# Factors ahead of the sum, gathers and the eighth load ahead of the key copies, and no drain on GpSimd's queue: attention and a routed mixture of experts on one core

## Chip, cores and metric

The kernel runs on one core of one Trainium2 chip. The metric is the device time of one execution in microseconds (us). The engines are TensorE (PE, matmuls and transposes; PEld is its weight load), VectorE (DVE), ScalarE (ACT), GpSimd (POOL) and SyncE (SP), which only issues DMAs here. GpSimd issues DMAs too: the casting loads of weights, the gathers and scatters by index, and some stores.

## What is computed

Blockwise causal attention over 8 batches, 8 heads, 576 positions and 64 features, then a layer of experts. Every position picks one of 8 experts, or, by a local gate, keeps the expert of the position before it.

```python
scores = np.where(block_i >= block_j, scale * q @ k.T, -1e9)     # blocks of 64
x = softmax(scores) @ v                                           # (8, 576, 512)
logits = x @ w_gate                                               # (8, 576, 8)
local_gate = sigmoid(x @ w_local)
for b, s:
    fresh_e = argmax(logits[b, s])
    e = fresh_e if s == 0 or local_gate[b, s] < 0.5 else prev_e
    h = relu(x[b, s] @ w1[e])                                     # 512 -> 1024
    out[b, s] = softmax(logits[b, s])[e] * (h @ w2[e])            # 1024 -> 512
```

## The kernel before

**Attention, 32 pairs.** The main loop (L1201) takes two heads at a time: 4 pairs a batch, 32 pairs, numbered from 0. Iteration i does on TensorE the value products of pair i−1 (L1000, L1009, tile `o`), the scores of pair i (L979, `sc`) and the transposes of the keys and queries of pair i+1 (L695, tile `kq`). ScalarE makes the exponentials `S` and `Pc`. VectorE adds the chunks of `Pc` to `S` (`add_chunks`, L1021 and L1023), so that one product with `sel` gives the row sums; a memset of a corner of `S` (`mask`, L1028) goes ahead of that product. `half_batch` (L708, tile `trg`) makes gate products (with `wg`) and these sums (with `sel`) for two pairs at a time.

**Keys.** `load_qk(i + 2)` (L869) issues the loads of keys and queries on SyncE's queue into a staging area; `arrange(i + 2)` (L882) copies each of the two, on GpSimd, into another part of that area, from which the transposes read. The areas are the places of the last two second-layer weights, experts 6 and 7. Even and odd pairs take turns, but pairs 29, 30 and 31 all use the last one, as expert 6 is loaded by then. So the loads of pair 31 wait until the copies of pair 30 have read.

**Routing.** While pairs run, VectorE and TensorE work through a generator of steps (`early`, L1056) with weights; `vector` lets it run as many VectorE steps as the numbers in AHEAD_OF, AFTER and END allow, and `END` is the credit at the end of an iteration by its number modulo 4. For the first five batches (groups 0 and 1) it computes each position's expert and rank (`tokens`), the probability of the expert (`factors_of`, L402) and then (`slots_first`, L456) the indices `idx0` of 15 tiles of 128 rows, each for one expert. These sums by one-hots run through L518 and L521 on VectorE and L531 on TensorE, at pair 28.

**Rows.** The attention's rows, divided by their sums (`rows_of_batch`, L821), are staged in `xg` or `x` and stored to `x_rows` in memory; each row has its factor in a last column, stored by separate DMAs from `factors` (L1255) that are kept in a list `held_f`. The six buffers of `xg` are also where the gathers (L653) bring a tile's rows. The list `pending` holds the first four gathers and the load of the eighth expert's first layer (L107); it is emptied on GpSimd at the end of iteration 28. The second layer of that expert (L111) is loaded at the end of iteration 30.

**Experts, 38 tiles.** 15 tiles come from the first five batches (phase 0), 23 and a conditional few from all that is left (phase 1). Per tile: a gather on GpSimd, a transposing DMA on SyncE's queue (`xT`, L1372), a copy of the expert's first layer on VectorE (`w1c`, L1359; for tiles 0 and 1 L1082), 32 matmuls (`ps_h`, L1097), relu, 8 matmuls (`ps_y`, L1303), scaling, and a scatter (L1314). Tile i's second product stands behind tile i+1's first. Beside tiles 1 to 13 the routing of the last three batches runs in the same way (`late`, L1322): `point` is called three times a tile and adds EACH to a credit. The indices `idx1` of phase 1 are its end, and the gather of tile 15, the first of phase 1, waits for that.

All engines run their instructions in the order in which the program lists them; semaphores make them wait for one another. DMAs issued by GpSimd share one queue.

Of the kernel before, what the change touches and what calls it, by code (L numbers as in the profile page):

```python
# [62 lines left out]
def kernel(  # L63
# [11 lines left out]
    nc = tc.nc  # L75
# [11 lines left out]
    E = moe_w_gate.shape[1]  # L87
# [27 lines left out]
    HP = H // 2  # L115
# [340 lines left out]
    def slots_first(T, TM, A):  # L456
# [82 lines left out]
                       + [lambda: load_weights(E - 1, 0)])  # L539
        nc.vector.tensor_copy(pay[:, NT:, ROW1], row1[:, 0, ns:])  # L540
        yield "V", 0.6
        yield from factors_of(*GROUPS[1], TM)
        yield "V", 0.6
        experts_of(0, te, TX)
        yield "V", 1.3

# [285 lines left out]
    with tc.tile_pool(name="atn_const", bufs=1) as cst, \  # L832
# [223 lines left out]
        def early():  # L1056

            while clock[0] < 4:
                yield None
            yield from constant_steps(T1)  # L1060
            yield "V", 1
            for j in range(2):

                while clock[0] < HP * GROUPS[j][1] // NC + 1.5:
                    yield None
                c0, c1 = GROUPS[j]
                TT = scratch_of_weights(0, E - 2)
                yield from tokens(c0, c1, TT, (TT, M1)[j], A1[:, c0:c1])
                if j == 0:
                    yield "V", 0.7  # L1070
                    yield from factors_of(c0, c1, TT)
            yield "V", 1
            yield from slots_first(S1, M1, A1)

# [72 lines left out]
        wload = 0  # L1147


        AHEAD_OF, AFTER, END = (0.6, 0.4, 0.4, 0.8), (0.4, 0.8, 0.4, 1.4), (1.7, 1.6, 1.5, 1.8)  # L1150

        left = [0]

# [22 lines left out]
        def behind(i):  # L1176

            def between():
                if i % HP == 2 and i < NPAIR - 2 or not routing(i) and i > 1:
                    vector(AHEAD_OF[i % HP])  # L1180
                run(sums)
                if sums:
                    routing(i)

            sums = sums_of(i)
            if sums:
                values(i - 1, between)
            else:
                values(i - 1)
                between()  # L1190
            if not swap:
                add_chunks(i - 1)
            if i == NPAIR - 2:
                mask(i - 1, nc.vector)
            load_v(i + 1)
            if i > 1:
                vector(AFTER[i % HP])
# [3 lines left out]
        for i in range(NPAIR):  # L1201
# [45 lines left out]
                routing(i)  # L1247
            if i < NPAIR - 1:
                vector(END[i % HP])
            arrange(i + 2, [nc.gpsimd.tensor_copy] * 2)  # L1250
            if i != NPAIR - 2:
                mask(i - 1, nc.gpsimd)
            for dst, src, made in held_f[:2 if i < HP * (NB1 + 2) else None]:
                if made < i or i == HP * (NB1 + 2):
                    nc.sync.dma_start(out=dst, in_=src)  # L1255
                    held_f.pop(0)
            if pending and i >= HP * (NB1 + 2):
                release(queue=nc.gpsimd)
            while pending and i >= HP * (NB1 + 2):
                pending.pop(0)()  # L1260

            if wload < 2 * E - 2 and i == min(2 + 2 * wload, HP * (NB1 + 2) - 1):
                load_weights(*divmod(wload, 2))
                wload += 1
            if i < NPAIR - 1:
                release(queue=nc.gpsimd)
            if i == NPAIR - 2:

                free = bf(Sb[(NPAIR - 3) % NSB], 2 * S * 2)[:, -AHEAD * Dm:]
                xTs = {}  # L1270
                for j in range(AHEAD):
                    xTs[j] = free[:, j * Dm:(j + 1) * Dm].rearrange("p (k n) -> p k n", k=KO1)
                    nc.sync.dma_start(out=xTs[j], in_=row_of_x(xgs[j]), transpose=True)
                load_weights(E - 1, 1)
        assert not pending
        clock[0] = NPAIR
        release()
        holding[0] = False


        nc.gpsimd.drain()

        values(NPAIR - 1)
        half.clear()
# [10 lines left out]
    with tc.tile_pool(name="ffn_s", bufs=2, reuse_waits="tile") as f_p, \  # L1295
# [54 lines left out]
                points[0] = 0  # L1350
            credit[0] -= spent

        EACH, ROWS_AT = 0.8, 4
        credit, points = [0], [0]
        chain, others = Steps(late()), Steps(rows())
        def weights_of(i):
# [136 lines left out]
```

## Time and profile before

| | us |
|---|---|
| median of 3 runs | 410.55 |
| lowest, highest | 410.48, 417.23 |
| the profiled execution | 411.95 |
| its span, first to last instruction | 409.9 |

The profile is of one execution. A row of the order of time has start, duration, engine, line, operation, what is written and read, count, and in brackets how long the engine was idle before it and what ended that. In a row of waits stand the engine and line that waited, what for, the total in us, how often, and the longest. A row of a stretch has start and end, then the busy us of PE, PEld, DVE, ACT and POOL with counts, the granted TensorE clock (1.00 is full), the DMA engines' share and GB/s. In the stretch from 0 to 240 us TensorE is busy almost throughout; 240 to 250 has it busy for 6.93 us at a mean clock of 0.83, 310 to 320 for 7.71 at 0.95. The profile names both layers' weights `w_bf`, both index tables `idx`.

### The profile page before, as it was taken

The numbers are of one execution on the slowest core, as the hardware profiler recorded it, in microseconds if no ns is written. First come the engines' busy times: TensorE is split into PE (matmuls) and PEld (weight loads), VectorE is DVE, ScalarE is ACT, GpSimd is POOL, SyncE is SP. The second block draws the span as 40 slices with busy tenths as digits, with TensorE's granted clock in tenths as the row PEclk, the third lists the DMA queues.
The fourth block names the chain that finished last, engine by engine and source line by source line (L and its number), as shares of the span: only waits on it lengthen the run. The fifth ranks groups of instructions, "written<-read, shape, count | busy, mean of one in ns | idle before, by whom it ended". The sixth has DMA issues, their size and how long they took to land. (4 is left out here: it accounts for less than half of the span.)

```text
span 409.9 us, 14501 instructions
## 1 busy us (share of the span) xinstructions
PE 393.1 (96%) x5827; PEld 285.4 (70%) x5827; DVE 239.0 (58%) x468; ACT 226.8 (55%) x390; POOL 187.2 (46%) x240
## 2 busy tenths in 40 slices
PE   8999999999999999998999979999998999999975
PEld 7677777776776776766777647677775777777753
DVE  3443756547577886469799646787894234433220
ACT  4667666665666665557556645444454355555442
POOL 1345255144154163341443272176866567766613
PEclk9999999999999999999999999999999899999998
DMA  6589999998988979989899979677552744565432
GB/s 182 135 191 231 206 175 240 203 185 227 214 162 236 203 155 201 187 193 217 157 211 224 180 171 173 116 138 176 138 153 87 157 143 130 150 149 142 125 88 78
DMA packets 111539, 69.97 MB, mean 171 GB/s; under 512 B 77567, under 2 KB 102975, under 8 KB 111472
## 3 DMA queue, kind: packets, MB, share of 16 engines
q0 software_dynamic: 18880, 34.83, 41.4%
q1 hardware_dynamic: 92592, 34.20, 35.4%
q8 instruction: 48, 0.79, 0.8%
q14 instruction: 19, 0.16, 0.1%
HBM read 66.88 MB, written 14.70 MB: 199 GB/s over the span
## 5 line engine op out<-in xcount | busy, mean ns | idle before, releaser
L882 POOL COPY w_bf<-w_bf 128x512 f32<-128x512 f32 x61 | 48.6, 812 | 106.8 <-DMA w_bf<-in_k_dram 75.5
L1021 DVE TENSOR_TENSOR S<-S,Pc 128x896 f32<-128x896 f32 (+2 forms) x96 | 84.7, 882 | 20.5 <-PE o L1000 16.0
L979 PE MATMUL sc<-qkT 64*64 64x224 f32 (+6 forms) x1536 | 90.1, 364 | 0.0
L1359 DVE COPY w1c<-w_bf 128x4096 bf16 x36 | 44.7, 1246 | 59.4 <-PE ps_h L1097 34.2
L1097 PEld LDWEIGHTS <-w1c 128*128 128x128 bf16 x1152 | 68.1, 98 | 12.6 <-issue 5.8
L1100 ACT ACTIVATE hT<-ps_h 128x512 bf16<-128x512 f32 x76 | 44.7, 598 | 52.2 <-PE ps_h L1097 32.3
L1303 PE MATMUL ps_y<-w_bf,hT 128*128 x304 | 72.4, 382 | 0.3 <-issue 0.3
L1097 PE MATMUL ps_h<-xT,w1c 128*128 128x128 bf16 x1088 | 67.8, 220 | 4.5 <-DMA xT<-xg 2.3
L979 PEld LDWEIGHTS sc<-qkT 64*64 64x64 f32 x1536 | 70.0, 133 | 1.2 <-ACT Pc L989 0.2
L653 POOL DMA_INDIRECT xg<-x_rows,idx x38 | 50.3, 1324 | 43.3 <-issue 17.8
L989 ACT ACTIVATE Pc<-sc 128x448 f32<-128x448 f32 (+1 forms) x96 | 68.2, 715 | 1.2 <-issue 1.1
L1314 POOL DMA_INDIRECT out_dram<-y,idx x38 | 46.0, 1210 | 26.1 <-issue 9.4
L1000 PE MATMUL o<-Pc,v 128*64 128x320 f32 (+2 forms) x512 | 57.4, 366 | 0.0
L1000 PEld LDWEIGHTS o<-Pc,v 128*64 128x64 f32 x512 | 35.3, 137 | 23.4
L989 ACT ACTIVATE S<-sc 128x576 f32<-128x576 f32 x64 | 42.0, 656 | 12.2 <-PE sc L979 12.2
L1303 PEld LDWEIGHTS <-hT 128*128 128x128 bf16 x304 | 28.6, 99 | 28.6 <-issue 1.8
L1311 ACT ACTIVATE y<-ps_y,xg 128x512 f32<-128x512 f32 (+1 forms) x38 | 25.9, 683 | 25.5 <-PE ps_y L1303 19.0
L1013 ACT COPY oT<-o 128x576 f32<-128x576 f32 x32 | 20.5, 641 | 34.1 <-PE o L1009 34.0
L1000 PE MATMUL o<-S,v 128*64 128x192 f32 (+1 forms) x256 | 34.8, 392 | 1.1 <-ACT Pc L989 0.8
L717 ACT COPY LT<-trg 128x320 f32<-128x320 f32 x15 | 6.4, 426 | 48.6 <-PE trg L708 48.6
L821 DVE TENSOR_TENSOR xg<-trx,rs 128x512 bf16<-128x512 f32 (+1 forms) x31 | 20.2, 684 | 19.3 <-PE trx L695 19.0
L948 ACT COPY qkT<-kq 128x1024 f32<-128x1024 f32 x30 | 30.8, 1028 | 0.4 <-PE kq L695 0.4
(273 smaller groups left out, 424.1 us busy)
## 6 DMA issues: line engine op xcount, KB each, us to landing
w_bf<-in_moe_w_dram POOLq DMA_DIRECT2D x16, 1024.0 KB
w_bf<-in_k_dram SPq DMA_DIRECT2D x32, 256.0 KB
w_bf<-in_q_dram SPq DMA_DIRECT2D x32, 256.0 KB
v<-in_v_dram SPq DMA_DIRECT2D x64, 128.0 KB
x_rows<-xg POOLq DMA_DIRECT2D x24, 128.0 KB
qkl<-in_k_dram SPq DMA_DIRECT2D x32, 32.0 KB
qkl<-in_q_dram SPq DMA_DIRECT2D x32, 32.0 KB
vl<-in_v_dram SPq DMA_DIRECT2D x32, 32.0 KB
```

Source lines behind the costliest of these rows:

```text
L653: st = nc.gpsimd.indirect_dma_start(out=x, out_offset=None, in_=x_dram[:rows], in_offset=bass.IndirectOffsetOnAxis(ap=row_of(ph, j), axis= ...
L882: copies[j](m, raws[i][1 + j].rearrange("p h j d -> p j h d"))
L948: nc.scalar.copy(to.rearrange("p a (r s) -> p r a s", r=2), ps.rearrange("p r (a s) -> p r a s", a=2))
L979: nc.tensor.matmul(to[:, col + skip:col + n], lhsT=t[r, 0, k0:k0 + ST], rhs=t[r, 1, q0 + skip:q0 + n], start=True, stop=True)
L989: nc.scalar.activation(exps_at(i, c, q0, n, rows), ps[rows, :, col:col + n], func=AF.Exp, scale=scale_attn)
L1000: nc.tensor.matmul(po[64 * h:64 * h + 64, VO + q0:VO + q0 + n], lhsT=vs[i][c][:, h, :], rhs=exps_at(i, c, q0, n, slice(0, P))[:, h, :], st ...
L1021: nc.vector.tensor_add(Ss[i][:, :, P * c:], Ss[i][:, :, P * c:], Pc[i % 2][:, :, POS[c]:POS[c] + n])
L1097: nc.tensor.matmul(ps[:, fo, :], lhsT=w[:, ko * F + f0:ko * F + f0 + P], rhs=xT[:, ko, :], start=(ko == 0), stop=(ko == KO1 - 1))
L1100: relu[0] = nc.scalar.activation(hT[:, half * (FO // 2):(half + 1) * (FO // 2), :], ps, func=AF.Relu)
L1303: nc.tensor.matmul(ps, lhsT=hT[:, fo, :], rhs=w2_bf[:, bass.ds(ev + fo * Dm, Dm)], start=(fo == 0), stop=(fo == FO - 1))
L1314: st = nc.gpsimd.indirect_dma_start(out=out_flat, out_offset=bass.IndirectOffsetOnAxis(ap=row_of(ph, j), axis=0), in_=y, in_offset=None, b ...
L1359: ended["w"] = nc.vector.tensor_copy(w, w1_bf[:, bass.ds(ev[i], WE)])
```

## The change

- The factors of group 1 (batches 3 and 4) are computed right behind its tokens, ahead of `slots_first`, and not behind the sum that gives the first indices. Their four stores go out two by two at the ends of iterations 26 and 27.
- At the end of each iteration the memset goes ahead of the key copies on GpSimd. For iterations 28 to 30 it is VectorE's, behind the chunk sums.
- At the end of iteration 28 the row store, the four gathers and the load of the eighth expert's first layer go ahead of the copies of pair 30.
- The load of that expert's second layer goes ahead of the row stores of iteration 30.
- No drain ahead of the last values. END has 2.4 for 1.6, EACH 1.0 for 0.8.

```diff
         nc.vector.tensor_copy(pay[:, NT:, ROW1], row1[:, 0, ns:])
         yield "V", 0.6
-        yield from factors_of(*GROUPS[1], TM)
-        yield "V", 0.6
         experts_of(0, te, TX)
...
                 yield from tokens(c0, c1, TT, (TT, M1)[j], A1[:, c0:c1])
-                if j == 0:
-                    yield "V", 0.7
-                    yield from factors_of(c0, c1, TT)
+                yield "V", 0.7
+                yield from factors_of(c0, c1, (TT, M1)[j])
             yield "V", 1
             yield from slots_first(S1, M1, A1)
...
-        AHEAD_OF, AFTER, END = (0.6, 0.4, 0.4, 0.8), (0.4, 0.8, 0.4, 1.4), (1.7, 1.6, 1.5, 1.8)
+        AHEAD_OF, AFTER, END = (0.6, 0.4, 0.4, 0.8), (0.4, 0.8, 0.4, 1.4), (1.7, 2.4, 1.5, 1.8)
...
-            if i == NPAIR - 2:
+            if HP * (NB1 + 2) <= i < NPAIR - 1:
                 mask(i - 1, nc.vector)
...
-            arrange(i + 2, [nc.gpsimd.tensor_copy] * 2)
-            if i != NPAIR - 2:
+            if i < HP * (NB1 + 2) or i == NPAIR - 1:
                 mask(i - 1, nc.gpsimd)
-            for dst, src, made in held_f[:2 if i < HP * (NB1 + 2) else None]:
-                if made < i or i == HP * (NB1 + 2):
-                    nc.sync.dma_start(out=dst, in_=src)
-                    held_f.pop(0)
             if pending and i >= HP * (NB1 + 2):
                 release(queue=nc.gpsimd)
             while pending and i >= HP * (NB1 + 2):
                 pending.pop(0)()
+            arrange(i + 2, [nc.gpsimd.tensor_copy] * 2)
+            for dst, src, made in held_f[:2]:
+                if made < i:
+                    nc.sync.dma_start(out=dst, in_=src)
+                    held_f.pop(0)
+            assert i < HP * (NB1 + 2) or not held_f
...
                 load_weights(*divmod(wload, 2))
                 wload += 1
+            if i == NPAIR - 2:
+                load_weights(E - 1, 1)
             if i < NPAIR - 1:
                 release(queue=nc.gpsimd)
...
-                load_weights(E - 1, 1)
...
-        nc.gpsimd.drain()
...
-        EACH, ROWS_AT = 0.8, 4
+        EACH, ROWS_AT = 1.0, 4
```

The order on GpSimd from the end of iteration 27 to the end of iteration 30, before. `xg_97` is the tile `xg`, `x_4028` and `x_4030` are two buffers of `x`, and the copies are the key copies of pairs 30 and 31:

```order
L680 DMA x_rows<-xg_97 128x256 x2
L882 COPY w2_bf_59<-w2_bf_59 128x512 x2
L1028 MEMSET S_104 64x2x64
L680 DMA x_rows<-xg_97 64x256
L653 DMA xg_97<-x_rows,idx0_89 128x257 x4
L107 DMA w1_bf_58<-in_moe_w1_dram 128x4x1024
L882 COPY w2_bf_59<-w2_bf_59 128x512 x2
L1028 MEMSET S_104 64x2x64
L680 DMA x_rows<-x_4028 128x256
L680 DMA x_rows<-x_4030 128x256
L680 DMA x_rows<-xg_97 64x256
L111 DMA w2_bf_59<-in_moe_w2_dram 128x8x512
```

The same place after the change (its lines are numbered two lower):

```order
L678 DMA x_rows<-xg_97 128x256 x2
L678 DMA x_rows<-xg_97 64x256
L651 DMA xg_97<-x_rows,idx0_89 128x257 x4
L107 DMA w1_bf_58<-in_moe_w1_dram 128x4x1024
L880 COPY w2_bf_59<-w2_bf_59 128x512 x4
L111 DMA w2_bf_59<-in_moe_w2_dram 128x8x512
L678 DMA x_rows<-x_4028 128x256
L678 DMA x_rows<-x_4030 128x256
L678 DMA x_rows<-xg_97 64x256
```

Both pairs' key copies now stand behind the gathers and the load, the two memsets have left GpSimd, and the load from `in_moe_w2` stands ahead of the stores from `x`.

Further down the same queue, where phase 1 begins: the scatters of tiles 8 to 12 (`y` with its number, then the index table) and the first gathers by `idx1`, before:

```order
L1314 DMA out_0_dram<-y_4900,idx0_89 4608x512
L1314 DMA out_0_dram<-y_4971,idx0_89 4608x512
L1314 DMA out_0_dram<-y_5040,idx0_89 4608x512
L1314 DMA out_0_dram<-y_5126,idx0_89 4608x512
L653 DMA xg_97<-x_rows,idx1_90 128x257 x4
L1314 DMA out_0_dram<-y_5209,idx0_89 4608x512
```

and after, where `y_4922` is tile 8's:

```order
L1311 DMA out_0_dram<-y_4922,idx0_89 4608x512
L1311 DMA out_0_dram<-y_5006,idx0_89 4608x512
L651 DMA xg_97<-x_rows,idx1_90 128x257 x2
L1311 DMA out_0_dram<-y_5084,idx0_89 4608x512
L651 DMA xg_97<-x_rows,idx1_90 128x257
L1311 DMA out_0_dram<-y_5146,idx0_89 4608x512
```

The first gathers of phase 1 have moved from behind tile 11's scatter to behind tile 9's.

On VectorE, around the chunk sums of pair 26 (L1021, L1023) and up to the sums that give `idx0`, before:

```order
L518 TENSOR_TENSOR w1_bf_58<-io_r_75,w1_bf_58 128x240
L1021 TENSOR_TENSOR S_104<-S_104,Pc0_117 128x2x448
L1021 TENSOR_TENSOR S_104<-S_104,Pc0_117 128x2x320
L1021 TENSOR_TENSOR S_104<-S_104,Pc0_117 128x2x192
L1023 TENSOR_TENSOR S_104<-S_104 64x2x64
L521 TENSOR_TENSOR x_f_3487<-w1_bf_58,row1s_85 128x480
```

and after:

```order
L1019 TENSOR_TENSOR S_104<-S_104,Pc0_117 128x2x448
L1019 TENSOR_TENSOR S_104<-S_104,Pc0_117 128x2x320
L1019 TENSOR_TENSOR S_104<-S_104,Pc0_117 128x2x192
L1021 TENSOR_TENSOR S_104<-S_104 64x2x64
L518 TENSOR_TENSOR w1_bf_58<-io_r_75,w1_bf_58 128x240
L521 TENSOR_TENSOR x_f_3494<-w1_bf_58,row1s_85 128x480
```

The first one-hot (L518) has moved behind the chunk sums.

## The prediction

> **What bounds the kernel now.** I read the page first, then what TensorE waits for, then the order of time around those waits.
>
> ```profile
> span 409.9 us, 14501 instructions
> PE 393.1 (96%) x5827; PEld 285.4 (70%) x5827; DVE 239.0 (58%) x468; ACT 226.8 (55%) x390; POOL 187.2 (46%) x240
> ```
>
> TensorE (PE) is busy for 96% of the span, and the change takes no matmul away. So it can win only what TensorE idles, and what it runs at a lowered clock. The table of waits has three entries above 1 us for PE:
>
> ```profile
> PE trg L708 <- POOL S L1028: 3.5, 3, 3.1
> PE ps_h L1097 <- DMA xT<-xg: 2.3, 1, 2.3
> PE ps_h L1097 <- ACTq L1453: 2.2, 1, 2.2
> ```
>
> The third is at the extra-tile branch near the end, which isn't touched. The other two lie where the change works. The order of time on TensorE shows each, with a later undisturbed run of the same sums (261.93) for comparison:
>
> ```profile
> 233.98 0.66 PE L695 MATMUL kq<-id_f,w_bf 64*128 64x64 f32 x16
> 240.52 0.75 PE L708 MATMUL trg<-oT,wg 128*32 128x320 f32 x8
> 244.33 2.36 PE L708 MATMUL trg<-S,sel 128*32 128x320 f32 x16 [3.07 <-POOL S L1028]
> 246.79 0.90 PE L695 MATMUL kq<-id_f,w_bf 64*128 64x64 f32 x16
> ...
> 261.93 1.28 PE L708 MATMUL trg<-S,sel 128*32 128x320 f32 x16
> ...
> 318.24 2.88 PE L1097 MATMUL ps_h<-xT,w1c 128*128 128x128 bf16 x32 [2.29 <-DMA xT<-xg]
> 320.91 2.65 PE L1303 MATMUL ps_y<-w_bf,hT 128*128 x8
> 323.40 1.95 PE L1097 MATMUL ps_h<-xT,w1c 128*128 128x128 bf16 x32
> 325.19 1.89 PE L1303 MATMUL ps_y<-w_bf,hT 128*128 x8
> ```
>
> Both gaps cost more than their idle time, because the granted clock halves behind them (start, us, five engines, then clock):
>
> ```profile
> 244.00:245.00 1.00, 0.67 (x8) 0.33 (x12) 0.00 (x0) 0.00 (x0) 0.22 (x2) 0.50 0.58 70
> 319.00:320.00 1.00, 1.00 (x14) 1.00 (x12) 0.00 (x0) 0.00 (x0) 0.69 (x2) 0.52 0.83 197
> ```
>
> **What it can win.** Gap A, before the sums of pair 30: 3.07 idle, 2.36 − 1.28 = 1.08 on the sums and 0.90 − 0.66 = 0.24 on the key transposes, 4.4 us. Gap B, before tile 15: 2.29 idle, 2.88 − 1.95 = 0.93 and 2.65 − 1.89 = 0.76, 4.0 us. The two small waits for the same memset, 3.5 − 3.1 = 0.4 us. In all 8.8 us.
>
> Gap A goes because the memset of pair 28's sums moves to VectorE, ahead of the work that GpSimd does for the gathers. Gap B goes because a larger credit (EACH) ends the routing chain two tiles earlier: the first two phase-1 gathers stand behind the output of tile 9 instead of tile 11, and a tile takes at most 1.95 + 1.89 = 3.8 us by the last two rows above, so they come some 7 us earlier, against 2.29 us of lateness. Next in line are the later gathers, each with a tile's time behind the one before.
>
> **What it costs, part by part.** GpSimd in order of time, before:
>
> ```profile
> 218.29 0.91 POOL L111 DMA_DIRECT2D w_bf<-in_moe_w_dram  x1 [0.34 <-PE trx L695]
> 220.42 1.14 POOL L680 DMA_DIRECT2D x_rows<-xg  x2 [1.22 <-DVE xg L821]
> 226.49 0.62 POOL L882 COPY w_bf<-w_bf 128x512 f32<-128x512 f32 x1 [4.93 <-DMA w_bf<-in_k_dram]
> 228.69 0.72 POOL L882 COPY w_bf<-w_bf 128x512 f32<-128x512 f32 x1 [1.58 <-DMA w_bf<-in_q_dram]
> ...
> 235.94 1.10 POOL L653 DMA_INDIRECT xg<-x_rows,idx  x1 [5.68 <-DMA x_rows<-factors]
> 237.34 1.84 POOL L653 DMA_INDIRECT xg<-x_rows,idx  x1 [0.30 <-issue]
> ...
> 240.98 1.00 POOL L653 DMA_INDIRECT xg<-x_rows,idx  x1 [0.31 <-issue]
> 241.98 0.83 POOL L107 DMA_DIRECT2D w_bf<-in_moe_w_dram  x1
> 242.86 1.17 POOL L882 COPY w_bf<-w_bf 128x512 f32<-128x512 f32 x2
> 244.08 0.20 POOL L1028 MEMSET S<- 64x128 f32 x1
> ...
> 252.08 0.93 POOL L111 DMA_DIRECT2D w_bf<-in_moe_w_dram  x1
> ...
> 264.43 1.59 POOL L653 DMA_INDIRECT xg<-x_rows,idx  x1 [11.06 <-issue]
> ```
>
> *The factors earlier.* On SyncE's queue their four stores now go two by two ahead of the key loads of pairs 29 and 30; those loads, in place for 226.49 until now, are next wanted at 235.6 (below), so this is hidden. The wait of 5.68 us goes, and the first gather can start soon after its indices:
>
> ```profile
> 222.77 0.17 DVE L452 TENSOR_SCALAR idx<-x_f 128x15 int32<-128x15 f32 x1
> ```
>
> But the third and fourth gather write xg[2] and xg[3], from which the two stores issued at 220.42 still read, and those stand in GpSimd's DMA queue behind the 1 MB load issued at 218.29. What that queue moved in 213 to 222 and in 223 to 231 us (packets, MB, share):
>
> ```profile
> q0 software_dynamic: 609, 1.28, 79.2%
> ...
> q0 software_dynamic: 1080, 1.20, 81.1%
> ```
>
> In the first stretch an earlier load and two stores (1.05 + 0.26 = 1.31 MB) go through; in the second 1.20 MB of the next load and its two stores, again 1.31 MB. At 1.20 / 8 = 0.15 MB per us the rest needs until 231.8, and the third gather starts at about 232.3 (between 231 and 233.5), however early the first two ran.
>
> *The key copies behind the gathers.* Behind the third gather (1.0 to 1.84, I take 1.2) come a gap of 0.30, the fourth (1.0), the load (0.83) and only then the two key copies of pair 30 (0.62, 0.72): 232.3 + 1.2 + 0.3 + 1.0 + 0.83 + 0.62 = 236.2, and 236.9. TensorE wants them at 233.98 and would be through at 234.6; now it is through at 236.9 + 0.33 = 237.2. Loss 2.6, I take 3.0 for what one semaphore adds on either side (1.6 to 4.9 by the ends above). Before, these copies were made at 226 to 229, and hidden.
>
> *The clock behind this new gap.* Gap B's 2.29 us was enough for a halved clock, so I add gap A's 1.08 + 0.24 = 1.3 (0 to 1.7, gap B's). The Trainium skill, "TensorE: Matmul & The Clock Gate", section "Part 1: The HAM clock gate", has the clock fall after an idle window of about 3.4 us; by that no 3-us gap would halve it, and the sum would be 1.3 less. The trace disagrees with its 2.29.
>
> *The keys of pair 31.* Their loads wait for those copies, since both pairs use one staging area:
>
> ```profile
> 216.44 1.07 SPq L869 DMA_DIRECT2D w_bf<-in_k_dram  x1
> ...
> 232.58 1.33 SPq L869 DMA_DIRECT2D w_bf<-in_k_dram  x1
> ```
>
> They are issued at 236.2 instead of 232.58, just behind a 1 MB load instead of ahead of it. The nearest loads in such company are pair 30's: 216.44 to 226.49, 10.05 us. So k lands at 246.3 and the q copy ends at 236.9 + 10.05 + 0.7 = 247.6. TensorE comes there at 237.2, plus 244.33 − 3.07 − 234.6 = 6.6 of work, 1.28 of sums and 1.3 of slow clock: 246.4. Loss 1.0 (0 if the loads take under 9 us; 3.4 if two more).
>
> *The eighth load ahead of the row stores.* It now waits for pair 31's transposes (246.79 + 0.90) and goes ahead of the stores of x: 247.7 + 0.93 + 1.05/0.15 + 0.9 + about 1.5 for start and receipt = 258. VectorE's next rows write those same two buffers, at
>
> ```profile
> 255.19 1.28 DVE L821 TENSOR_TENSOR x<-trx,rs 128x512 bf16<-128x512 f32 x2
> 256.39 1.22 DVE L1082 COPY qkT<-w_bf 128x4096 bf16 x1
> 257.52 2.60 DVE L1021 TENSOR_TENSOR S<-S,Pc 128x896 f32<-128x896 f32 x3
> ...
> 260.04 1.96 PE L1097 MATMUL ps_h<-S,qkT 128*128 128x128 bf16 x32
> ```
>
> so they, and behind them on VectorE the copy of tile 1's weights and the last sums, come 2.8 later. The copy then ends at 260.4, tile 1 waits 0.4, and the sums for trg (261.93) another 1.3. Loss 1.7 (0 to 4, since the transposes of the first gathered tiles now also run beside that load).
>
> *Small ones.* One one-hot (L518) falls behind pair 26's sums, on the way to the first gathers' indices:
>
> ```profile
> 213.77 0.41 DVE L518 TENSOR_TENSOR w_bf<-io_r,w_bf 128x240 bf16<-128x240 f32 x1
> ```
>
> at most 0.41, I take 0.3. With EACH at 1.0 the chain crowds VectorE, busy 9.17 us (the third engine) of these ten:
>
> ```profile
> 280.00:290.00 10.00, 10.00 (x110) 7.16 (x108) 9.17 (x22) 5.26 (x9) 6.89 (x6) 1.00 0.64 141
> ```
>
> I take 0.4 (0 to 1). The drain is free: GpSimd's 11.06 idle us ahead of 264.43 hold nobody up on TensorE. The memsets ahead of the key copies, pair by pair, only trade places on an engine that waits for keys; END's larger credit likewise moves work within VectorE's idle time.
>
> Losses 3.0 + 1.3 + 1.0 + 1.7 + 0.3 + 0.4 = 7.7 against 8.8: 1.1 us faster. The profiled execution took 411.95, its span 409.9 and 2.05 around it; the median of the runs is 410.55, 1.4 lower. 411.95 − 1.1 = 410.85 there, and 409.5 on the scale of the median.
>
> **The rivals.**
> 1. *The stores of xg land early, or the copies aren't late.* Then new gap, clock and keys (5.3) fall away: 404.2, and 402.5 if the x buffers are free in time too (both stores late is one cause, the queue's rate), 401.8 if the small costs are nothing. For it: GpSimd idled 4.93 us ahead of 226.49, which the gathers would fill, and 0.15 MB per us was measured beside other traffic. Against it: the queue is busy at 81% of the engines in that stretch as it is. 0.28, of it 0.17 at 2% or past it.
> 2. *The keys of pair 31 come late* (slower than before). From a load time of 9 us on, each us is lost on TensorE; at 13, with a second halved clock, 3.9 + 1.3 instead of 1.0: 413.7. 0.18, a third of it with further waits behind, past 2%. For it: in 213 to 222 us, while a load of 2 KB rows ran, the queue of the keys moved little:
>
> ```profile
> q1 hardware_dynamic: 1126, 0.45, 22.1%
> ```
>
> The Trainium skill, "DMA: Bandwidth & Descriptors", section on queues, rings and completion order, has each DMA engine take turns between queues packet by packet. By that page 1 KB packets beside 2 KB ones get a third of the (1.28 + 0.45) / 9 = 0.19 MB per us, an estimate of 8 us for the 0.52 MB of both keys, short of that point.
>
> 3. *The clock stays up behind the new gap*: 1.3 less, 408.2. 0.09; the row of gap B speaks against it. It is also what the Trainium skill's rule in "TensorE: Matmul & The Clock Gate" would give.
> 4. *The chain isn't earlier*, because VectorE at 9.17 of 10 can't be fed faster: gap B stays, 413.5. 0.09.
>
> **How the numbers follow.** The forecast, new stalls in the place of the old ones, has 0.36. Rivals 1 to 4 make up the rest. Its own range, with the two largest terms at their ends, is 406 to 413. The range 402 to 415 takes in rival 1 and rivals 2 and 4 each alone; it leaves out the two together and what is worse, some 0.15. 2% (8.2 us) is about what a measurement of this kernel can tell from no change; 8.8 us of gain just reach it, with rival 1's 0.17. Slower by as much needs rival 2's last third, or rival 4 on top: 0.09. Within: 0.74.
>
> **What would show it.** Right: no idle ahead of trg near 244; an idle of some 3 us ahead of kq near 234, put down to a copy on GpSimd, whose third gather starts behind 231; a half clock after it; w1c, tile 1, late by 1 to 2 us; no wait for xT at tile 15. Wrong: all four gathers issued by 229, or the key copies of pair 30 done before 234; then rival 1 holds. A second gap ahead of the next kq is rival 2.

## The result and the profile after

| | median, us | runs | ratio to the kernel before, 95% interval |
|---|---|---|---|
| before | 413.89 | 410.48, 410.55, 417.23, 420.18 | |
| changed | 425.67 | 425.05, 425.34, 426.00, 428.14 | 1.038 [1.031, 1.045] |
| changed, on another chip (f0 below) | 427.24 | 423.22 to 431.55 | 1.029 [1.018, 1.040] |

Disturbed runs, two of the four of e1 among them, are left out of every ratio and of the medians of the kernel before that are given with the experiments. The kernel is slower by 3 to 4%, where the forecast was 1 us faster. The profiled execution took 426.0, its span 424.2; that of before was 409.9. From the page of the changed kernel:

```profile
span 424.2 us, 14452 instructions
PE 397.0 (94%) x5806; PEld 290.8 (69%) x5827; DVE 231.4 (55%) x470; ACT 225.7 (53%) x390; POOL 172.5 (41%) x238
```

The table of waits of the changed kernel. Neither the memset (3.5 us before) nor `xT` (2.3) is in it any more; the two at the top are new.

```profile
PE kq L693 <- POOL w_bf L880: 6.5, 1, 6.5
PE trg L706 <- DVE x L819: 4.0, 1, 4.0
PE ps_h L1094 <- ACTq L1450: 2.3, 1, 2.3
```

The order of time on TensorE, changed kernel: the first wait ahead of the keys of pair 30, no wait for those of pair 31 (255.17), the second wait, tile 1 at half clock, and tile 15 (331.36) with no wait.

```profile
237.10 0.24 PE L693 MATMUL o<-id_f,qkl 64*128 64x64 f32 x1 [0.15 <-DMA qkl<-in_k_dram]
238.17 0.27 PE L693 MATMUL o<-id_f,qkl 64*128 64x64 f32 x1 [0.83 <-DMA qkl<-in_q_dram]
244.96 1.24 PE L693 MATMUL kq<-id_f,w_bf 64*128 64x64 f32 x16 [6.51 <-POOL w_bf L880]
255.17 0.66 PE L693 MATMUL kq<-id_f,w_bf 64*128 64x64 f32 x16
...
271.58 0.75 PE L706 MATMUL trg<-oT,wg 128*32 128x320 f32 x8 [4.00 <-DVE x L819]
272.94 3.42 PE L1094 MATMUL ps_h<-S,qkT 128*128 128x128 bf16 x32 [0.62 <-DVE qkT L1079]
...
327.85 1.95 PE L1094 MATMUL ps_h<-xT,w1c 128*128 128x128 bf16 x32
331.36 1.95 PE L1094 MATMUL ps_h<-xT,w1c 128*128 128x128 bf16 x32
```

Laying the starts of the same instructions of the two profiles side by side gives the account of the 14.3 us. "Late" is the changed kernel's start less that of before; each row's share is the growth of that lateness.

| up to | late, us | share | what lies in it |
|---|---|---|---|
| scores of pair 1 | 1.55 | +1.55 | first loads, ahead of anything the change touches |
| scores of pair 29 | 3.01 | +1.46 | a wait of 1.18 for `qkl`, 0.72 for the one-hots of L521, others |
| scores of pair 30 | 12.79 | +9.78 | waits of 0.15, 0.83 and 6.51, then a halved clock |
| scores of pair 31 | 8.15 | −4.64 | gap A is gone |
| tile 1 | 12.90 | +4.75 | waits of 4.00 and 0.62 |
| tile 2 | 13.97 | +1.07 | tile 1 at half clock |
| tile 14 | 15.57 | +1.60 | tiles 6 to 11 later by 1.9, part given back |
| tile 16 | 11.48 | −4.09 | gap B is gone |
| end | 14.26 | +2.78 | 1.65 of it a halved clock that fell on the extra tile |

So both gains came in this execution, each to 0.2 us as forecast. The losses add up to 23 us, where 7.7 was forecast. The first and the last row are mostly luck: all profiles of the experiments are between 0.4 us early and 1.8 late at pair 1, and from tile 16 to the end they gain up to 0.9 or lose up to 3.7. The wait of 2.3 us at the extra tile was there before too (2.2), without a halved clock behind it. Without these two rows the losses are 18.7 us. GpSimd in order of time shows where the largest begins:

```profile
214.99 0.80 POOL L107 DMA_DIRECT2D w_bf<-in_moe_w_dram  x1
...
223.36 0.62 POOL L880 COPY w_bf<-w_bf 128x512 f32<-128x512 f32 x1 [2.34 <-DMA w_bf<-in_k_dram]
227.52 0.86 POOL L880 COPY w_bf<-w_bf 128x512 f32<-128x512 f32 x1 [3.54 <-DMA w_bf<-in_q_dram]
228.33 0.91 POOL L111 DMA_DIRECT2D w_bf<-in_moe_w_dram  x1
229.23 1.62 POOL L678 DMA_DIRECT2D x_rows<-xg  x3
...
232.56 1.02 POOL L651 DMA_INDIRECT xg<-x_rows,idx  x1 [0.30 <-issue]
241.15 1.00 POOL L651 DMA_INDIRECT xg<-x_rows,idx  x1 [7.57 <-DMA x_rows<-xg]
...
244.25 1.20 POOL L880 COPY w_bf<-w_bf 128x512 f32<-128x512 f32 x2
...
257.48 0.94 POOL L111 DMA_DIRECT2D w_bf<-in_moe_w_dram  x1 [3.08 <-PE trx L693]
```

The load of expert 6's second layer (L111) was issued at 218.29 before and is issued at 228.33 here. The two stores behind it (L678) land late with it, the third gather waits 7.57 for them, and the key copies of pair 30 stand behind that gather. The load is late because it stands behind the key copies of pair 29 (223.36 and 227.52; before 214.32, two in 2.48). SyncE's queue tells why those came late:

```profile
213.42 1.96 SPq L1256 DMA_DIRECT2D x_rows<-factors  x2
215.48 0.54 SPq L867 DMA_DIRECT2D w_bf<-in_k_dram  x1
216.11 0.41 SPq L867 DMA_DIRECT2D w_bf<-in_q_dram  x1
```

The loads of pair 29 go out at 215.48, behind two factor stores and half a us behind the issue of a 1 MB load (214.99 above). Before, they went out at 210.22, 2.2 us ahead of that load (212.39). Here are SyncE and then GpSimd of the kernel before:

```profile
210.22 0.54 SPq L869 DMA_DIRECT2D w_bf<-in_k_dram  x1
...
212.39 0.80 POOL L107 DMA_DIRECT2D w_bf<-in_moe_w_dram  x1
...
214.32 2.48 POOL L882 COPY w_bf<-w_bf 128x512 f32<-128x512 f32 x2
```

Of the 5.3 us by which the loads go out later, about 3 are TensorE's own lateness at pair 27 and 2 are the stores. From issue to copy the keys take 7.9 us instead of 4.1, and the queries 11.4.

Behind the 6.51 us the clock is halved, as forecast; it fell while TensorE still waited:

```profile
242.00:243.00 1.00, 0.00 (x0) 0.00 (x0) 0.00 (x0) 0.00 (x0) 0.70 (x2) 0.50 0.13 31
```

### The profile page after: what moved, and what is told of

It is laid out like the page before. It is cut to its first block, busy times and chain, and to the rows that moved or that the text cites. A ratio compares the mean times of both kernels' runs of the same rounds, so it can differ in the third digit from the quotient of the medians.

```text
span 424.2 us, 14452 instructions
## 1 busy us (share of the span) xinstructions
PE 397.0 (94%) x5806; PEld 290.8 (69%) x5827; DVE 231.4 (55%) x470; ACT 225.7 (53%) x390; POOL 172.5 (41%) x238
## 4 chain that ended last, share of the span: by engine, by line
PE 49%; issue 19%; POOL 14%; DMA 9%; DVE 5%; ACT 1%; POOLq 1%; SPq 1%; DVEq 0%; ACTq 0%
PE o L998 16%; PE sc L977 15%; POOL out_dram L1311 8%; PE trg L706 5%; POOL xg L651 5%; PE kq L693 3%; DMA v<-in_v_dram 3%; DMA x_rows<-x 3%; DVE S L1019 2%; DMA out_dram<-y,idx 2%; DMA w_bf<-in_q_dram 2%; PE o L1007 2%; PE ps_h L1094 2%; PE trx L693 1%; PE ps_y L1300 1%
## 5 line engine op out<-in xcount | busy, mean ns | idle before, releaser
L1019 DVE TENSOR_TENSOR S<-S,Pc 128x896 f32<-128x896 f32 (+2 forms) x96 | 80.1, 835 | 22.3 <-PE o L998 17.8
L977 PE MATMUL sc<-qkT 64*64 64x224 f32 (+6 forms) x1536 | 91.4, 367 | 0.0
L1094 PEld LDWEIGHTS <-w1c 128*128 128x128 bf16 x1152 | 68.1, 99 | 12.6 <-issue 4.5
L1300 PE MATMUL ps_y<-w_bf,hT 128*128 x283 | 68.4, 382 | 1.2 <-issue 0.2
L1026 POOL MEMSET S<- 64x128 f32 x28 | 5.6, 200 | 120.1 <-DVE S L1021 62.0
L1311 POOL DMA_INDIRECT out_dram<-y,idx x38 | 43.7, 1149 | 24.8 <-ACT y L1308 13.2
L880 POOL COPY w_bf<-w_bf 128x512 f32<-128x512 f32 x61 | 38.3, 650 | 36.7 <-DMA w_bf<-in_k_dram 21.3
L998 PEld LDWEIGHTS o<-Pc,v 128*64 128x64 f32 x512 | 36.7, 138 | 22.6 <-issue 0.6
L998 PE MATMUL o<-S,v 128*64 128x192 f32 (+1 forms) x256 | 35.9, 400 | 1.5 <-DMA v<-in_v_dram 1.0
```

Source lines behind the costliest of these rows:

```text
L880: copies[j](m, raws[i][1 + j].rearrange("p h j d -> p j h d"))
L977: nc.tensor.matmul(to[:, col + skip:col + n], lhsT=t[r, 0, k0:k0 + ST], rhs=t[r, 1, q0 + skip:q0 + n], start=True, stop=True)
L998: nc.tensor.matmul(po[64 * h:64 * h + 64, VO + q0:VO + q0 + n], lhsT=vs[i][c][:, h, :], rhs=exps_at(i, c, q0, n, slice(0, P))[:, h, :], st ...
L1019: nc.vector.tensor_add(Ss[i][:, :, P * c:], Ss[i][:, :, P * c:], Pc[i % 2][:, :, POS[c]:POS[c] + n])
L1094: nc.tensor.matmul(ps[:, fo, :], lhsT=w[:, ko * F + f0:ko * F + f0 + P], rhs=xT[:, ko, :], start=(ko == 0), stop=(ko == KO1 - 1))
L1300: nc.tensor.matmul(ps, lhsT=hT[:, fo, :], rhs=w2_bf[:, bass.ds(ev + fo * Dm, Dm)], start=(fo == 0), stop=(fo == FO - 1))
```

## The experiments

The kernels whose labels begin with e, c or f are the changed kernel with edits, those with b the kernel before with edits. They ran on several chips, and the kernel before ran beside them: its median was 411.05 beside e1 to e4, 412.27 beside e5, c1, c3 and b4, 416.08 beside e7, b1, b2 and b3, and 412.40 beside f0 to f3. So ratios are to be compared, not times.

**The keys of pair 30.** Four kernels ask whether the order on GpSimd makes the wait, and what makes its input late.

e1: the copies ahead of the gathers again.

```diff
+            arrange(i + 2, [nc.gpsimd.tensor_copy] * 2)
             if pending and i >= HP * (NB1 + 2):
                 release(queue=nc.gpsimd)
             while pending and i >= HP * (NB1 + 2):
                 pending.pop(0)()
-            arrange(i + 2, [nc.gpsimd.tensor_copy] * 2)
```

> The changed kernel with the two key copies of pair 30 ahead of the row store, the four gathers and the load again, as before; nothing else is undone. Theory A (the copies only stand in the wrong place in GpSimd's order: bytes on the key queue say that pair 30's keys had landed by about 231.5, and they were copied at 244.25): the copies come by 233, the idle time ahead of kq of pair 30 falls from 6.51 to under 1.0, no halved clock behind it, time 415 to 419 in place of 425.7. Theory B (the loads of those keys are themselves late beside the load of expert 6's second layer, so the order does not matter): copies after 238, at least 3 us idle ahead of kq, time 421 to 426.

It took 415.50 and 415.76. GpSimd and TensorE of e1:

```profile
233.39 1.32 POOL L880 COPY w_bf<-w_bf 128x512 f32<-128x512 f32 x1 [8.13 <-DMA w_bf<-in_k_dram]
235.63 0.83 POOL L880 COPY w_bf<-w_bf 128x512 f32<-128x512 f32 x1 [0.91 <-DMA w_bf<-in_q_dram]
```

```profile
237.80 0.71 PE L693 MATMUL kq<-id_f,w_bf 64*128 64x64 f32 x16
```

The copies follow the landing, and TensorE does not wait at all. Theory A: about 4.6 us over the kernel before are left of some 14. The copies are at 233.39 and 235.63 though, later than A's 233: the loads are not quick either.

e7: the two stores ahead of the second-layer load of iteration 27.

```diff
+            if i == HP * (NB1 + 2) - 1:
+                release(queue=nc.gpsimd)
             if wload < 2 * E - 2 and i == min(2 + 2 * wload, HP * (NB1 + 2) - 1):
                 load_weights(*divmod(wload, 2))
```

> The changed kernel with one pair swapped on GpSimd: the two stores from xg[2] and xg[3] in iteration 27 ahead of the 1 MB load of expert 6's second layer, not behind it. Theory A (the third gather waits only for those stores, and they only for that load): the third gather follows the second at once, at 233 to 235 in place of 241.15, the key copies of pair 30 come by 238, idle ahead of kq of pair 30 at most 2.0 in place of 6.5, time 416 to 420. Theory B (the stores land late for another reason): third gather after 238, time 422 to 427.

419.95 (417.47 to 424.92), ratio 1.011 [0.998, 1.024]. GpSimd of e7:

```profile
224.83 0.92 POOL L111 DMA_DIRECT2D w_bf<-in_moe_w_dram  x1
...
231.84 1.13 POOL L651 DMA_INDIRECT xg<-x_rows,idx  x1 [0.30 <-issue]
233.28 1.40 POOL L651 DMA_INDIRECT xg<-x_rows,idx  x1 [0.30 <-issue]
...
237.01 1.21 POOL L880 COPY w_bf<-w_bf 128x512 f32<-128x512 f32 x2
```

The third gather follows the second at once, and kq of pair 30 has no wait. Theory A: gather behind stores, stores behind the load. (The second copy ends at 238.22, where A had 238.)

f0: the changed kernel once more, on the chip of f1.

> The changed kernel once more, as the neighbour of the other three on the same chip. Both theories: 424 to 428, the third gather 12 to 14 us behind the issue of expert 6's second-layer load, and idle time ahead of kq of pair 30 of 3 to 7 us.

427.24; the load at 227.77, the third gather at 240.30, a wait of 3.86. Six profiles have the load ahead of the stores, the copies behind the gathers and the factor stores on SyncE ahead of the key loads. The third column says how far ahead of the scores of pair 28 on TensorE the load was issued (in the kernel before 3.9 us); the last is the time from the scores of pair 29 to those of pair 30 (in the kernel before 6.7 us).

| kernel | second-layer load issued | ahead of scores 28 | third gather | behind the load | idle ahead of kq | scores 29 to 30 |
|---|---|---|---|---|---|---|
| changed | 228.33 | −2.3 | 241.15 | 12.8 | 6.51 | 16.4 |
| e5 | 226.67 | −1.1 | 238.77 | 12.1 | 3.81 | 12.6 |
| e3 | 226.13 | 1.1 | 239.73 | 13.6 | 3.49 | 13.7 |
| f0 | 227.77 | 1.4 | 240.30 | 12.5 | 3.86 | 13.1 |
| f3 | 229.96 | 2.1 | 243.10 | 13.1 | 2.33 | 12.1 |
| e4 | 223.53 | 2.9 | 237.34 | 13.8 | 2.19 | 12.4 |

The delay behind the load hardly varies; what varies is the load's own place, and the idle time with it. The loss in this stretch is 5.5 to 9.8 us, where 3.0 and 1.3 were forecast.

e2 and f1 ask about the factor stores: e2 issues the last four behind the key loads, f1 on ScalarE's queue.

```diff
             load_qk(i + 2)
+            for dst, src, made in held_f[:2 if i > NPAIR - 6 else 0]:
+                if made < i - 1:
+                    nc.sync.dma_start(out=dst, in_=src)
+                    held_f.pop(0)
...
-            for dst, src, made in held_f[:2]:
+            for dst, src, made in held_f[:2 if i < NPAIR - 6 else 0]:
```

```diff
-                    nc.sync.dma_start(out=dst, in_=src)
+                    (nc.scalar if i >= NPAIR - 6 else nc.sync).dma_start(out=dst, in_=src)
```

> The changed kernel with the last four factor stores one place later on SyncE's queue: behind the key loads of pairs 29 and 30 and not ahead of them. Theory A (those stores held the loads of pair 29 until 215.48, half a us behind the issue of a 1 MB load at 214.99, and from there the load of expert 6's second layer was issued at 228.33 and not near 219, and the third gather ran at 241.15 and not near 233): loads of pair 29 issued by 213.6, both key copies done by 221, the 1 MB load issued by 222, third gather at 233 to 236, idle ahead of kq of pair 30 at most 3, time 417 to 422. Theory B (the loads are slow wherever they stand, since GpSimd's load is issued 1.5 us later anyhow): third gather after 239, idle over 5, time 424 to 427.

> The changed kernel with the last four factor stores issued on ScalarE's queue at the same place of the program, and not on SyncE's. Theory A (on SyncE they held the key loads of pair 29 until those fell beside the 1 MB load, so that GpSimd came to expert 6's second layer at 228.33): loads of pair 29 issued at least 1.5 us ahead of the 1 MB load of that iteration, the second-layer load issued by 222 plus the lateness that TensorE already has at pair 28, the third gather 12 to 14 us behind that, idle ahead of kq of pair 30 at most 2.5, time 417 to 422. Theory B (those loads fall beside the 1 MB load without the stores too): second-layer load after 224, idle over 3, time 423 to 427.

e2 423.77, ratio 1.029 [1.022, 1.036]; f1 423.99, ratio 1.023 [1.015, 1.031]. In both the load keeps its place relative to TensorE: it is issued 3.7 us ahead of the scores of pair 28 (224.56 against 228.23, 225.14 against 228.81). In f2 (below), which has the stores on ScalarE too, it is 4.4 us ahead. With the stores on SyncE ahead of the key loads it is anywhere between 2.3 us behind them (the changed kernel) and 3.7 ahead (e1). So the stores push it by up to 6 us, in most executions but not in all. The times missed A all the same, since a cost comes back in the next place. GpSimd of e2:

```profile
224.56 0.90 POOL L111 DMA_DIRECT2D w_bf<-in_moe_w_dram  x1
...
241.94 1.09 POOL L651 DMA_INDIRECT xg<-x_rows,idx  x1 [12.66 <-DVE S L1021]
```

Now the first gather waits 12.66. The profile names VectorE, which had long been done; the factor stores were issued at 231.17 here, and the gathers read what they write. On TensorE e2 loses 6.0 us from the scores of pair 28 to those of pair 29, with waits of 1.00 and 2.87 for `v`, and 2.7 more to those of pair 30. In f1 the first gather came at 236.99 and the idle time ahead of kq was 0.88, but the scores of pair 30 still came 11.0 us behind those of pair 29. Stores early enough for the gathers are in the way of the key loads; stores behind the key loads are late for the gathers.

**The eighth load.** e3 puts it back behind the row stores.

```diff
-            if i == NPAIR - 2:
-                load_weights(E - 1, 1)
...
                     nc.sync.dma_start(out=xTs[j], in_=row_of_x(xgs[j]), transpose=True)
+                load_weights(E - 1, 1)
```

> The changed kernel with the second-layer load of the eighth expert behind the row stores of iteration 30 again, as before. Theory A (the stores of the two x buffers land only behind that load, VectorE waits 6.25 us for them, and TensorE 4.0 ahead of trg and 0.62 ahead of tile 1, with a halved clock behind): the idle time ahead of trg goes to under 0.5, time 418 to 422. Theory B (another wait stands right behind it, as the transposes of the gathered tiles beside those stores, or the weights of the eighth expert arrive late for a tile): at least 3 us idle somewhere between 260 and 290, time 424 to 427.

415.64, ratio 1.013 [1.005, 1.020]. VectorE of the changed kernel, and then of e3, at the row that writes the two x buffers:

```profile
269.95 1.48 DVE L819 TENSOR_TENSOR x<-trx,rs 128x512 bf16<-128x512 f32 x2 [6.25 <-DMA x_rows<-x]
```

```profile
262.09 1.28 DVE L819 TENSOR_TENSOR x<-trx,rs 128x512 bf16<-128x512 f32 x2
```

The wait is gone, and TensorE has none between 260 and 270. Theory A, with a time below its range. From pair 31 to tile 2 the lateness falls by 0.4 us, where the changed kernel's grows by 5.8. The rest of the 10 us isn't this edit's: the profiled execution came to pair 31 1.5 us less late, and from tile 16 on gained 0.7 where the changed kernel lost 2.8.

**EACH.** e4 has 0.8 for 1.0.

> The changed kernel with EACH at 0.8 as before, in place of 1.0. Theory A (the larger credit took away the wait at tile 15, 4.0 us with its halved clock, and cost some 2 us of late weight copies in tiles 5 to 11): the wait at tile 15 is back, time 426 to 429. Theory B (the routing chain is early enough either way, since the other changes moved it too): no idle at tile 15, tiles 5 to 11 quicker, time 423 to 425.

420.05, ratio 1.025 [1.019, 1.031]: out of A's range and of B's. Its waits:

```profile
PE kq L693 <- POOL w_bf L880: 2.2, 1, 2.2
PE ps_h L1094 <- DMA xT<-xg: 2.2, 1, 2.2
```

The wait at tile 15 is back, so A's mechanism holds; the time is low in part because of the short wait for keys (table above), and the clock did not halve behind the wait at tile 15. From the first product of tile 2 to that of tile 16 e4 takes 56.1 us, the kernel before 58.1, the changed one 55.6, e1, e2, e3 and e5 55.9 to 56.0, and f0 56.3. So beside e4 EACH at 1.0 is worth half a us at most; it would be more where the wait is followed by a halved clock, as in the kernel before.

**The memset behind the copies.** e5 undoes that for iterations up to 27.

```diff
-            if i < HP * (NB1 + 2) or i == NPAIR - 1:
-                mask(i - 1, nc.gpsimd)
...
             arrange(i + 2, [nc.gpsimd.tensor_copy] * 2)
+            if i < HP * (NB1 + 2) or i == NPAIR - 1:
+                mask(i - 1, nc.gpsimd)
```

> The changed kernel with the memset behind the two key copies again in iterations up to 27; all else stays changed. Theory A (ahead of the copies it waits 9 to 10 us for the chunk sums and keeps landed keys waiting: copies at 147.45 in place of 144.29; the weight load behind them is issued later, the factor stores of that batch fall beside its data and take 5.06 us of SyncE in place of 2.16, and the v loads behind them come late): TensorE waits for v under 1 us in all ahead of pair 28, time 421 to 424. Theory B (END at 2.4, or the factor stores themselves, are the cause): waits for v of 1 to 9 us remain in the pairs 9 to 28, time 424 to 427.

423.33, ratio 1.031 [1.021, 1.041]: within A's range, but beside the changed kernel's 1.029 and 1.038 no difference can be told by the time. The profiles say more. In e5 TensorE has no wait for `v` ahead of pair 28, as A said. Here is SyncE at the end of one batch, in the kernel before and then in e1, where the memset stands ahead:

```profile
152.21 2.16 SPq L1255 DMA_DIRECT2D x_rows<-factors  x2
154.47 0.58 SPq L869 DMA_DIRECT2D w_bf<-in_k_dram  x1
```

```profile
153.13 5.06 SPq L1256 DMA_DIRECT2D x_rows<-factors  x2
```

and TensorE of e1 ten us on:

```profile
163.12 1.67 PE L998 MATMUL o<-S,v 128*64 128x192 f32 x8 [2.46 <-DMA v<-in_v_dram]
```

A wait of over 2 us for `v` at this pair is in seven of the ten profiles that have the memset ahead (e1, e2, e4, c1, f0, f1, f3; not in the changed kernel's first one and e3, and 1.22 in e7), and in none of six that have it behind (before, e5, c3, f2, b1, b3). Theory A's place is right. That the wait comes by way of the factor stores is argued from SyncE's order and not shown by itself, and e5's time does not confirm the size.

**Undone together.** c1 is e1 and e3, c3 is e1, e3 and e5. f2 is c3 with the factor stores on ScalarE and the drain back.

> Two edits undone together: pair 30's key copies ahead of the gathers, and the eighth second-layer load behind the row stores. If the two losses are independent (8 to 10 us and 6 to 10 us by the single runs, from 425.7): 406 to 412, with waits for v of 2 to 5 us left in the pairs ahead of 28. If the second only moves what the first leaves (rival): 413 to 416.

> The three edits undone together: pair 30's key copies ahead of the gathers, the eighth second-layer load behind the row stores, the memset behind the key copies. What stays of the change: factors ahead of the sum, memsets of the last pairs on VectorE, no drain, END 2.4, EACH 1.0. Theory A (these three are the whole loss, and the gains of the two removed waits, 4.4 and 4.0 less 1 to 2, are real): 402 to 407. Theory B (the earlier factors or END cost of their own): 408 to 413.

> A candidate: key copies of pair 30 ahead of the gathers, the eighth second-layer load behind the row stores, memsets up to iteration 27 behind the copies, the drain back, the last four factor stores on ScalarE's queue. Stays changed: factors ahead of the sum, the last memsets on VectorE, END 2.4, EACH 1.0. If the gains of the two removed waits can be had at all: 1 to 2% faster than the kernel before. If the DMA queue of that stretch sets the pace whatever the order (rival): within 0.5% of the kernel before.

c1 417.21, ratio 1.010 [1.001, 1.019]; c3 413.29, ratio 1.002 [0.996, 1.009]; f2 416.16, ratio 1.005 [1.000, 1.010]. The waits of c3:

```profile
PE o L998 <- ACT qkT L946: 1.8, 1, 1.8
PE ps_h L1094 <- ACTq L1449: 1.5, 1, 1.5
PE trg L706 <- DVE S L1026: 1.2, 1, 1.2
```

Neither new wait is left. (c1 has one more, 2.79 ahead of the first `ps_y`, which its profile puts down to a gather.) So those three edits together are the loss of the change; how much of it is the memset's (1.010 to 1.002) isn't clear of the noise. By its ratio, on the scale of 411, c1 stands at 415, in the rival's range, and c3 at 412, which is Theory B: what stays is worth nothing together. f2 is its rival's case. No version here is faster than the kernel before by more than the noise.

The gains are there in the profiles all the same. From the scores of pair 29 to those of pair 31 the kernel before takes 20.1 us, e1 16.0, c1 16.4 and c3 18.2, and from tile 2 to tile 16 c3 takes 55.7 for 58.1. But the profiled execution of c3 was 4.1 us late at pair 29, and that of b3 below, which is the kernel before up to there, was 3.0 late. So how late an execution comes to pair 29 varies by as much as the gains, also without the change. Whether what stays of the change makes it later isn't shown.

**The gains alone.** b1 is the kernel before with the memsets of iterations 28 to 30 on VectorE, b2 with EACH at 1.0, b4 with both.

> The kernel before with the memsets of iterations 28 to 30 on VectorE, nothing else. Theory A (the wait of 3.07 us for the memset is worth what the prediction gave it, 4.4 and 0.4 of the other two): 4 to 5 us faster than the kernel before on the same chip. Theory B (the DMA queue is what bounds this stretch: the last second-layer load lands at 261.8 and the first ps_y runs at 263.56, so TensorE only comes earlier to a wait for that load): at most 2 us faster, with a new idle time of 2 to 3 us ahead of the first ps_y.

> The kernel before with EACH at 1.0, nothing else. Theory A (the wait at tile 15 with its halved clock, 4.0 us, goes; tiles 5 to 11 lose about 1.5 to late weight copies): 2 to 3 us faster than the kernel before, no idle ahead of tile 15. Theory B (the crowded VectorE eats it all): within 1 us.

> The kernel before with two parts of the change alone: the memsets of the last pairs on VectorE, and EACH at 1.0. The wait of 3.07 ahead of trg and that of 2.29 at tile 15 go, with the halved clock behind each: 8.8 less 1 to 2 of late weight copies, so 403 to 405 beside 411 for the kernel before. Rival (GpSimd's copies or loads behind the gathers are late next, as the memset was only the first of them): 407 to 411.

b1 ratio 0.996 [0.991, 1.001], b2 0.996 [0.990, 1.001], b4 1.007 [1.001, 1.012]. Of 416 us, 0.4% is 1.7 us, and the interval of b1 ends at 3.6, where removing gap A was to give 4.8: Theory A is out. The time is within Theory B's, but the idle time that B had ahead of the first `ps_y` isn't there. b2 lies between its two theories. b4 is slower than both of its own, and slower than b1 and b2, which isn't explained. TensorE's waits of b1 between 236 and 250 us, and two of its us:

```profile
PE sc L977 <- issue: 1.2, 2, 0.8
PE sc L979 <- issue: 0.4, 1, 0.4
```

```profile
241.00:242.00 1.00, 0.22 (x2) 0.10 (x1) 0.00 (x0) 0.00 (x0) 1.00 (x3) 1.00 0.88 208
243.00:244.00 1.00, 0.88 (x10) 0.40 (x12) 0.00 (x0) 1.00 (x3) 0.10 (x1) 0.50 0.73 70
```

While the four gathers run (236.08 to 241.1), TensorE's instructions trickle: it waits for nothing that the profile shows, and the clock is halved behind that too. From the scores of pair 30 to those of pair 31 b1 takes 13.76 us; the kernel before, with gap A in it, takes 13.40. In this execution the gap only changed its name. Neither theory had this, and why e1 and c1 could use the time and b1 could not is open.

**The drain.** b3 is the kernel before without it, f3 the changed kernel with it.

> The kernel before without the drain on GpSimd, nothing else. Theory A (as predicted: nobody on TensorE waits for it): within 1 us of the kernel before, gathers behind it some us earlier. Theory B (gathers and their transposes that start earlier take bandwidth from the last second-layer load, for which the first ps_y waits): 1 to 3 us slower.

> The changed kernel with the drain put back, nothing else. Theory A (the drain holds nobody): within 1 us of the changed kernel. Theory B (without it the next gathers run beside the last second-layer load and delay it, as the kernel before without the drain measured 0.7% slower): 2 to 4 us faster.

b3 ratio 1.007 [1.003, 1.011], that is 1 to 4.5 us slower. f3 ratio 1.023 [1.012, 1.035] beside f0's 1.029 [1.018, 1.040], which tells nothing apart. b3 is in Theory B's range by its time, but its profile, with the next gather at 258.64 in place of 264.43, has no new wait on TensorE there. Its lateness is 3.00 at pair 29 already, ahead of the drain's place, 3.14 at tile 0 and 2.81 still at tile 30; the rest of its 5.8 us comes from tile 31 on. What the drain does for the kernel stays open.

## Why the prediction was wrong

By its own steps:

- *What it can win*: right in size for this execution. Gap A −4.64 (4.4 and 0.4 forecast), gap B −4.09 (4.0). It isn't a price that holds everywhere: with gap A's memset alone moved, b1 gains 3.6 us at most by its interval.
- *The key copies behind the gathers*: the mechanism was right (third gather behind two stores, those behind a 1 MB load, copies behind the gather; e1 and e7). The term was mis-sized: 3.0 and 1.3 of clock forecast, 9.78 measured, and 5.5 to 7.0 in five other profiles. The step that failed is "The factors earlier … so this is hidden". It took the issue of the load from the profile of before (218.29) and asked only when pair 30's keys are wanted. But the factor stores also go ahead of pair 29's key loads, whose copies stand ahead of that load on GpSimd. These copies came 9 to 12 us later than before, with TensorE itself 3 to 4 late, and the load 6.2 us later relative to TensorE. With the stores out of the way (e2, f1, f2) the load is in its old place; with them it is up to 6 us later, by the execution. Where it is only 1.0 later (e4), the term is 5.8.
- *The eighth load ahead of the row stores*: right mechanism, size too small: 1.7 forecast, 5.8 measured (4.75 and 1.07), and e3 gives it back. The sum counted the 1 MB from an issue at 247.7, at 0.15 MB per us; it was issued at 257.48, with TensorE 8.15 late, and VectorE's row came 12.5 us behind that (269.95) where the sum had 10.3. Its 1.5 for start and receipt has no row behind it. And the halved clock behind the new wait wasn't counted.
- *The keys of pair 31* (1.0; by the sum's own terms, 247.6 against 246.4, it is 1.2): no wait; TensorE was 8 us late itself by then. Rival 2, the one that would have been slower, did not happen; rivals 1 and 4 are out by the third gather at 241.15 and by tile 15 without a wait.
- *L518 behind the chunk sums* (0.3): 0.72 in the row of L521. *EACH* (0.4): 1.6 by tile 14.
- *The memsets … only trade places*: in seven of ten profiles a wait for `v` of over 2 us stands against it, though not in the profiled execution above.
- *The drain is free*: not shown; b3 speaks against it.
- *The clock behind the new gap*: halved, so rival 3 is out. The rule of the Trainium skill, "TensorE: Matmul & The Clock Gate", section "Part 1: The HAM clock gate" (a window of about 3.4 us), would halve it behind 6.51 as well, so this run does not tell the two apart. Gap B's 2.29 and the other profiles do: 2.0 us of idle time were enough where they lay in one such window (last section). That the 3-us gap would halve the clock couldn't be known from its length.

The signs that would have shown it wrong did not come: the shape was as drawn, and the range failed on two sizes. The 4.3 us of the first and the last row of the account can be put down to luck; without them the time would still lie outside the range. One cause can be argued for both sizes: the costs were read from the timetable of the kernel before, and in the new one the same transfers start later and beside others.

## What to carry to other kernels

When a step is moved ahead on one queue, follow every transfer behind it to the engine that waits for it, and what that engine has queued behind the wait: here two stores that held SyncE for 2 us pushed a load on GpSimd, two hops later, by up to 6 us. Don't put work with a deadline (key copies) behind work that waits for memory (a gather), even if the engine idles, or see first that the gather has nothing to wait for (the stores of e7). And a removed wait is worth its length only if the engine can run in that time: b1 spent it in slow issue (13.76 us for 13.40), while e1 and c1 gained 4.1 and 3.6 over the scores of pairs 29 to 31.

## What the runs showed of the hardware that was not expected

Two waits of nearly the same length for `v` at the same pair had different sequels. These are the ten us from 160 in e1 (a wait of 2.46) and in c1 (2.53):

```profile
160.00:170.00 10.00, 7.54 (x91) 5.38 (x94) 3.59 (x6) 3.00 (x6) 3.00 (x6) 0.83 0.74 121
```

```profile
160.00:170.00 10.00, 7.47 (x128) 5.93 (x124) 5.83 (x8) 4.69 (x8) 3.15 (x5) 1.00 0.78 162
```

In e1 the clock went to 0.50 behind it, in c1 it stayed at 1.00, also behind a later wait of 2.79. In every profile the halved stretches last 3.41 us or twice that, except at the end. Within one profile they also all begin a whole number of 3.413 us apart, so time can be cut into windows of that length that don't follow the program.

What TensorE idles in one window sorts the cases. Over the 18 profiles, without the first 12 and the last 15 us, all 30 windows at full clock with 1.96 us idle or more were followed by a halved one, 9 of 61 with 1.0 to 1.96, and 1 of 1899 with less. The wait of e1 lies in one window (2.46). That of c1 is cut in two (1.39 and 1.14), and so are its wait of 2.79 (1.4 and 1.4) and e4's of 2.16 at tile 15 (1.66 and 0.50). Gap B's 2.29 lay in one. So whether a gap of 2 to 3 us costs a halved stretch depends on where it falls.

TensorE's instructions trickled while gathers ran in b1, f1 and f2 (idle times put down to "issue" of 0.2 to 0.8), but not in e1, c1 or e7, which run the same four gathers at 230 to 248. What decides it wasn't found.
